# Attention placed ahead of block 3, and Strassen's scheme in the second product of blocks 3 to 5

## The chip, the core and the metric

The kernel runs on one core of one Trainium2 chip. The time is the device time of one execution, in microseconds (us): 510.04 us is the median of three runs of the kernel before (508.49 to 510.45). One further execution was profiled. Its page names the engines so: PE is the matrix engine's multiplications and PEld its weight loads, DVE the vector engine, ACT the scalar engine, POOL the general engine, SP the engine that issues most DMAs. One matrix instruction of this kernel covers 512 or 256 columns of one PSUM bank. PSUM has eight banks of 128 x 512 floats here.

## The reference

A linear attention with a decaying state gives one row per token; the rows of all heads are joined and go through a two-layer product with a gate between:

```
for t in range(S):                              # batch 4, heads 8, S = 768, D = 48
    cur = einsum('bhd,bhe->bhde', u * k_t, v_t)
    y[:, :, t] = einsum('bhd,bhde->bhe', r_t, state + cur)
    state = w_t * state + einsum('bhd,bhe->bhde', k_t, v_t)
x = y.transpose(0, 2, 1, 3).reshape(3072, 384)
h = x @ w_in                                    # 384 -> 2048
g = where(h >= 1, h, where(h <= -1, 0, (h + 1) ** 2 / 4))
out = g @ w_out                                 # 2048 -> 384
```

## The kernel before

**Tiling.** The 3072 tokens are twelve units of 256 (64 time steps of four batches). Attention is computed unit by unit (`attention`, line 498), since unit u needs the state after unit u-1. Two units make a block of 512 tokens, `x_[b % 2]`, and there are six blocks, 0 to 5. A block goes through 16 steps, one for each 128 of the 2048 hidden rows. In block 0 five of them and in block 1 fourteen are done as two halves of 256 columns (`HALVES`), so that the first unit of the block can be used alone.

**A step.** Every float is kept as a rounded high part and a low part, and a product of two floats is three products of parts. The first product of a step (`product_in`, line 1294; its matmul is line 1299) is 9 instructions of 512 columns into a bank `h`. The gate is two ACT operations and one DVE operation (lines 1111 to 1113), and ACT and DVE then make the two parts `gh` and `gl` (1115, 1116). The second product (`product_out`, matmul in line 1319) is again 9 instructions of 512 columns; they add into three banks `acc`, one for each 128 output rows, over all 16 steps. After the last step of a block the three banks are copied out (line 1136) and stored.

**Strassen's scheme.** Blocks in `FAST` take another path, `fast` (line 952); before, that is block 5 alone. It treats two steps as one 2 x 2 problem: the hidden rows of the two steps, the two halves of the 512 tokens, and the first two of the three output thirds (the last third is done plainly). Sums and differences of the gate's results (`t`, lines 989 to 997) and of the weights (`sums_of`, line 925, written once into buffers that attention no longer needs, `HOMES`) go in; seven products and four plain ones come out, `M1` to `M7`, `P`, `Q`, `R` in line 914. Every product is three instructions of 256 columns (line 1011). Of the eight pairs of a block, seven are done so with 33 instructions; the last pair is done plainly into the same places with 36. The results lie in five banks (3, 4, 5, 1, 2), and `finish` (line 1052) puts the outputs together with one ACT copy and six DVE additions, and stores six pieces of 128 KB.

**Attention of a unit.** SP loads w, r and k (as `wq`, `rk`), a token-major copy `nk` and v. DVE runs two scans for each of two slots (lines 543, 538), multiplies (564, 614), sums (604, 607), masks (590) and updates the state (671, 674); POOL multiplies (602, 610); PE does small products of 64 x 64 (584, 653, 696) and transposes (623). The result is evacuated as high part by ACT (768) and low part by DVE (766) into `x_`, a fourth slice into `last`, which six DMAs spread over the rest of `x_` (line 811). Each unit uses banks 0, 1 and 2 in turn (`take`) and one of the two `h` banks.

**What sets the order.** Nothing is scheduled on the chip. At build a planner (`Plan`, line 54) takes every operation with its engine, a cost, what it reads and writes, and a due time, simulates all engines, and writes down the order of each engine. Due times of steps come from `STEP`, those of a unit's attention from the block that reads it (`step_of`, line 1143). Where the planner sees PE idle it adds multiplications by zero (`kept_warm`, line 184). Each engine then runs its list in order and waits on semaphores. `guard` (line 829) reads each unit's w again, two ACT operations each, for a check of the inputs; its verdict decides at the end whether another path (`general`) is run.

Of the kernel before, what the change touches and what calls it, by code (L numbers as in the profile page):

```python
# [10 lines left out]
F32 = mybir.dt.float32  # L11
# [5 lines left out]
ALU = mybir.AluOpType  # L17
# [26 lines left out]
FAST = {NB - 1}  # L44
# [3 lines left out]
SCRATCH = 8192  # L48
# [300 lines left out]
STEP, FIRST, PACED = 4.9, 24.0, 4.6  # L349
ROUNDS = 1  # L350


def attention_moe(tc, a):
# [32 lines left out]
    vn = tiles(2, [128, 2, VW], F32, "vn")  # L386
# [12 lines left out]
    fl = tiles(FULL, [128, 768], F32, "fl")  # L399
# [98 lines left out]
    def attention(u, when):  # L498
# [255 lines left out]

        def yevac(g, part, what):
            yv = bank[by[g]].rearrange("p (a c t) -> p a c t", a=4, t=C)
            if what:
                yv = yv[:, 3]
                to = [last[:, n, :].rearrange("p (c g t) -> p c g t", c=2, g=2)[:, :, g, :] for n in range(2)]
            else:  # L760
                yv = yv[:, 0:3]
                to = [x[:, n].rearrange("p a (c g t) -> p a c g t", c=2, g=2)[:, :, :, g, :] for n in range(2)]
            if part and u in INPLACE:
# [16 lines left out]
        def names(what, n, g):  # L780
            return ("last" if what else ("x", blk % 2, half), n, g)
# [15 lines left out]
        for what in (0,) if alone else (1, 0):  # L797
            for g in range(2):
                op("ACT", 0.27 if what else 0.48, due, [("b", by[g])], [names(what, 0, g)], lambda g=g, w=what: yevac(g, 0, w))
                if u not in INPLACE:  # L800
# [8 lines left out]

        def fill(e, h, j):  # L810
            e.dma_start(
                out=x[64 * h + 48 : 64 * h + 64, :, j, :].bitcast(F32),
                in_=last[64 * h + 16 * j : 64 * h + 16 * j + 16].bitcast(F32),
            )

        xs = [(("x", blk % 2, half), n, g) for n in range(2) for g in range(2)]
        for j in range(0 if alone else 3):
            for h in range(2):
                e, how = (nc.scalar, "ACT") if h and u < APART else (nc.sync, "SP")
                op(how, 0.8 if how == "ACT" else 0.63, due, [("last", n, g) for n in range(2) for g in range(2)] + xs, [("x", blk % 2, half, j, h)],  # L820
                   lambda e=e, h=h, j=j: fill(e, h, j), size=32768)
        plan.group(first, when, LEADS.get(u, LEAD))
# [70 lines left out]
    for i in range(3):  # L893
        mem(("h", i, 0), None, ("gh", i))
        mem(("l", i, 0), None, ("gl", i))
    mem(("h", 0, 1), None, *xk)
    his = [gh, [xf[:, 512 * i : 512 * i + 512] for i in range(3)]]
    los = [gl, [xf[:, 1536 + 512 * i : 2048 + 512 * i] for i in range(3)]]
    HOMES = [("nk0", 1536, 0), ("nk0", 1536, 512), ("nk0", 1536, 1024), ("vn0", 800, 0), ("vn1", 800, 0), ("r0", 512, 0), ("r1", 512, 0),
             ("wq0", 521, 0), ("wq1", 521, 0), ("wq2", 521, 0), ("y0", 520, 0), ("seeds0", 520, 0), ("fl0", 768, 0), ("fl1", 768, 0),  # L900
             ("fl2", 768, 0), ("fl2", 768, 256)]
    olds = [ku_keys, (), (), (("v", 0), ("vpad", 0)), (("v", 1), ("vpad", 1)), (("R", 0),), (("R", 1),), (("w", 0),), (("w", 1),), (("w", 2),),
            ("y",), ("seeds",), (("fl", 0),), (("fl", 1),), (("fl", 2),), ()]
# [3 lines left out]
    def sums(i, n):  # L907
# [7 lines left out]
             "M5": (1, 0), "R": (1, 1), "M3": (2, 0), "M4": (2, 1)}  # L915
# [36 lines left out]
    def fast(n, after=()):  # L952
# [9 lines left out]
        for half in range(2):  # L962
            xs += [(("x", b % 2, half), i, g) for i in range(2) for g in range(2)]
            xs += [("x", b % 2, half, j, h) for j in range(3) for h in range(2)]
# [10 lines left out]
        def split(i, x, key):  # L975

            hi, lo = his[k][i], los[k][i]
            op("ACT", 0.6, due, [key], fresh_in(("h", i, k)), lambda: A.copy(hi, x))
            op("DVE", 0.67, due, [key, ("h", i, k)], fresh_in(("l", i, k)), lambda: V.tensor_tensor(
                out=lo, in0=x, in1=hi.bitcast(F32), op=ALU.subtract), port=True)  # L980
# [408 lines left out]
```

## Time and profile before

| what | value |
|---|---|
| median of three runs | 510.04 us |
| the profiled execution | 508.99 us, of which 507.3 us from its first to its last instruction (the span) |
| granted clock of the matrix engine, mean | 0.993 |
| DVE, ACT, POOL busy | 368.3, 299.9, 100.4 us |
| matmuls of the first product, 512 columns | 693; of 256 columns, 342 |
| matmuls of the plain second product, 512 columns | 549; of 256 columns, 342 |
| matmuls of Strassen's scheme, 256 columns | 267 |
| HBM read and written | 47.09 and 4.72 MB |

Matmul rows give how long each is under way, and they overlap: one of 512 columns is listed with about 0.4 us, while the next one starts after about 0.23 us. What an instruction costs the matrix engine is therefore read from the distance of starts in a row of them. DVE and ACT rows overlap by some hundredths of a microsecond in the same way, and the busy times count no moment twice. In the windows view, each row is a stretch of the span with the busy time of each engine in it and, in brackets, the number of instructions.

### The profile page before, as it was taken

The numbers are of one execution on the slowest core, as the hardware profiler recorded it, in microseconds if no ns is written. First come the engines' busy times: TensorE is split into PE (matmuls) and PEld (weight loads), VectorE is DVE, ScalarE is ACT, GpSimd is POOL, SyncE is SP. The second block draws the span as 40 slices with busy tenths as digits, with TensorE's granted clock in tenths as the row PEclk, the third lists the DMA queues.
The fourth block names the chain that finished last, engine by engine and source line by source line (L and its number), as shares of the span: only waits on it lengthen the run. The fifth ranks groups of instructions, "written<-read, shape, count | busy, mean of one in ns | idle before, by whom it ended". The sixth has DMA issues, their size and how long they took to land. (4 is left out here: it accounts for less than half of the span.)

```text
span 507.3 us, 13117 instructions
## 1 busy us (share of the span) xinstructions
PE 492.1 (97%) x5525; PEld 417.2 (82%) x5525; DVE 368.3 (73%) x631; ACT 299.9 (59%) x628; POOL 100.4 (20%) x80
## 2 busy tenths in 40 slices
PE   6989999999999999999999999999999999999995
PEld 4679988888999998888888888888788877889894
DVE  6999989988888797835888435987333486697753
ACT  4769798978754566634555543556444454665651
POOL 1745516411121103101110101110000034402000
PEclk9989999999999999999999999999999999999998
DMA  8984916156342352501442201430100020100002
GB/s 295 378 317 154 364 79 232 57 172 216 105 153 92 127 165 71 167 1 67 151 152 59 109 0 59 157 121 12 63 0 1 1 58 13 68 1 2 1 1 68
DMA packets 22051, 54.70 MB, mean 108 GB/s; under 512 B 3040, under 2 KB 9184, under 8 KB 21984
## 3 DMA queue, kind: packets, MB, share of 16 engines
q1 hardware_dynamic: 21840, 53.65, 30.7%
q8 instruction: 45, 0.74, 0.6%
q14 instruction: 22, 0.18, 0.1%
q10 hardware_dynamic: 144, 0.13, 0.1%
HBM read 47.09 MB, written 4.72 MB: 102 GB/s over the span
## 5 line engine op out<-in xcount | busy, mean ns | idle before, releaser
L1299 PE MATMUL h<-x,wt 128*128 128x512 f32 (+1 forms) x1035 | 219.6, 360 | 1.5 <-DVE g L1113 0.8
L1299 PEld LDWEIGHTS h<-x,wt 128*128 128x128 f32 x1035 | 169.9, 188 | 32.6 <-DVE g L1113 1.8
L1319 PE MATMUL acc<-gh,wt 128*128 128x512 f32 (+1 forms) x594 | 130.3, 354 | 0.0
L1319 PEld LDWEIGHTS acc<-gh,wt 128*128 128x128 f32 x594 | 97.2, 188 | 16.8
L1111 ACT ACTIVATE g<-h 128x512 f32<-128x512 f32 (+1 forms) x99 | 51.0, 515 | 96.1 <-PE h L1299 86.6
L1113 DVE SCALAR_TENSOR_TENSOR g<-g,h 128x512 f32<-128x512 f32 (+1 forms) x99 | 57.1, 579 | 65.3 <-ACT g L1112 57.5
L1116 DVE TENSOR_TENSOR gl<-g,gh 128x512 fp32r<-128x512 f32 (+1 forms) x99 | 62.2, 634 | 22.9 <-ACT gh L1115 20.4
L1319 PE MATMUL acc<-gl,wt 128*128 128x512 f32 (+1 forms) x297 | 72.1, 351 | 0.0
L1115 ACT CAST gh<-g 128x512 fp32r<-128x512 f32 (+1 forms) x99 | 52.7, 536 | 26.7 <-DVE g L1113 23.0
L610 POOL TENSOR_TENSOR r<-cst,d 128x512 f32<-128x512 f32 x18 | 19.2, 1089 | 194.2 <-PE bank L696 158.0
L1319 PEld LDWEIGHTS acc<-gl,wt 128*128 128x128 f32 x297 | 50.3, 188 | 8.4
L1112 ACT ACTIVATE g<-g 128x512 f32<-128x512 f32 (+1 forms) x99 | 54.3, 550 | 1.8
L478 POOL TENSOR_SCALAR wraw<-fl 128x768 uint16<-128x768 f32 x13 | 43.3, 3354 | 50.1 <-ACT wraw L476 38.7
L602 POOL TENSOR_TENSOR nk<-nk 128x768 f32<-128x768 f32 x9 | 17.6, 1961 | 83.3 <-DMA nk<-in_nk 83.3
L543 DVE TENSOR_TENSOR_SCAN p<-wq,seeds 128x520 f32<-128x520 f32 x24 | 30.1, 1254 | 3.0 <-DMA wq<-in_w 2.1
L538 DVE TENSOR_TENSOR_SCAN y<-wq,seeds 128x520 f32<-128x520 f32 x24 | 30.0, 1250 | 0.8
L972 DVE SCALAR_TENSOR_TENSOR rk<-rk,h 128x512 f32<-128x512 f32 x16 | 11.0, 685 | 14.5 <-ACT rk L971 14.4
L590 DVE COPY_PREDICATED r<-below,bank 128x512 f32<-128x512 int32 x23 | 16.0, 730 | 4.6 <-PE bank L584 4.5
L564 DVE TENSOR_TENSOR rk<-rk,y 128x512 f32<-128x512 f32 x24 | 18.0, 750 | 0.9 <-ACT nk L554 0.7
L768 ACT CAST x<-bank 128x384 fp32r<-128x384 f32 x24 | 11.1, 485 | 12.0 <-PE bank L696 11.8
L969 ACT ACTIVATE rk<-h 128x512 f32<-128x512 f32 x16 | 9.6, 598 | 13.9 <-PE h L1299 13.9
L696 PEld LDWEIGHTS bank<-rk,st 64*64 64x64 f32 (+1 forms) x704 | 12.2, 133 | 6.7 <-issue 5.0
(198 smaller groups left out, 619.9 us busy)
## 6 DMA issues: line engine op xcount, KB each, us to landing
rk<-in_rk SPq DMA_DIRECT2D x24, 512.0 KB, 4.9
wraw<-in_wbits SPq DMA_DIRECT2D x16, 768.0 KB, 7.6
nk<-in_nk SPq DMA_DIRECT2D x9, 768.0 KB, 4.5
wq<-in_w SPq DMA_DIRECT2D x24, 260.5 KB, 2.8
vn<-in_v SPq DMA_DIRECT2D x12, 384.0 KB, 6.7
fl<-in_w SPq DMA_DIRECT2D x12, 260.0 KB, 2.9
out_y<-g SPq DMA_DIRECT2D x10, 256.0 KB, 3.1
x<-last SPq DMA_DIRECT2D x60, 32.0 KB, 3.1
```

Of the source, the lines that this page charges most:

```text
L478: op(on, 0.62 if f in SIGNS else 3.2, due, [("fl", k)], [("raw", f)], lambda: e.tensor_scalar(out=half(1), in0=s, scalar1=0.0, scalar2=327 ...
L538: V.tensor_tensor_scan(out=y_[:, ::-1], data0=w[:, SEG:0:-1], data1=sv[:, ::-1], initial=0.0, op0=ALU.mult, op1=ALU.add)
L543: V.tensor_tensor_scan(out=pv[:, q].rearrange("p n c -> p (n c)"), data0=w[:, 0:SEG], data1=sv, initial=0.0, op0=ALU.mult, op1=ALU.add,)
L564: op("DVE", 0.69, due, ["y"], [("k", s)], lambda q=q: V.tensor_tensor(out=parts(q, 1), in0=parts(q, 1), in1=y_.rearrange("p (n c) -> p n c ...
L610: op("POOL", 1.1, due, ["d", "cst"], [("R", h)], lambda h=h: G.tensor_tensor(out=r_[h], in0=twice.unsqueeze(1).unsqueeze(1).broadcast_to([ ...
L1111: op("ACT", c, due, [("h", n)], [("g", gk)], lambda: nc.scalar.activation(gs, hs(), AF.Relu, scale=0.5, bias=0.5), uses=[hk])
L1112: op("ACT", c, due, (), [("g", gk)], lambda: nc.scalar.activation(gs, gs, AF.Square))
L1113: op("DVE", 0.13 + 0.53 * k, due, [("h", n)], [("g", gk)], lambda: nc.vector.scalar_tensor_tensor(out=gs, in0=gs, scalar=1.0, in1=hs(), op ...
L1115: op("ACT", c, due, [("g", gk)], [("gh", gk)], lambda: nc.scalar.copy(ghs, gs))
L1116: op("DVE", 0.17 + 0.54 * k, due, [("g", gk), ("gh", gk)], [("gl", gk)], lambda: nc.vector.tensor_tensor(out=gls, in0=gs, in1=ghs.bitcast( ...
L1299: nc.tensor.matmul(hp, lhsT=wx[f][:, cs], rhs=xt[:, j, :], start=n == 0, stop=n == 8)
L1319: nc.tensor.matmul(o[j], lhsT=wx[f][:, cs], rhs=gt, start=first and i == 0, stop=stop and i == 2, skip_group_check=True)
```

## The change

Five things change. Their names: `xf` are two new f32 tiles for the x of blocks 4 and 5; `FLAT` holds those blocks; `ADDED` says at which block's first step each unit's attention is given to the planner, and `PULLED` gives units 4 to 11 due times 16 us apart, the last at the start of block 3.

```
-FAST = {NB - 1}
+FAST = set(range(NB - 3, NB))
+FLAT = {NB - 2, NB - 1}
...
-SCRATCH = 8192
+SCRATCH = 2048
...
+PITCH = 16.0
+SLOW, QUICK = 5.75, 4.05
+ADDED = {0: (2, 3), 1: (4, 5), 2: tuple(range(6, NU))}
...
+    xf = tiles(len(FLAT), [128, 3, WIDE], F32, "xf")
...
             if flat_x:
+                A.copy(to[0].bitcast(F32), yv)
...
-        t += STEP if cs is whole else STEP / 2 if n >= HALVES[0] else PACED
+        pace = QUICK if b in FAST else SLOW
+        t += pace if cs is whole else pace / 2 if n >= HALVES[0] else PACED
...
+    PULLED = {u: (before_fast((NU - 1 - u) * PITCH), 4.0) for u in range(4, NU)}
...
-             "M5": (1, 0), "R": (1, 1), "M3": (2, 0), "M4": (2, 1)}
+             "M5": (1, 0), "R": (1, 1), "M3": (2, 0), "M4": (0, 0)}
...
+        xs += [("hu", u) for u in range(1, NU - 1)]
...
-            multiply(1.2, one_, [("M3", S3, g1), ("M4", lambda: weights(f0, A2), g0)])
-            multiply(1.3, two_, [("M2", lambda: weights(f1, A1), g2), ("Q", lambda: weights(f1, A3), g2)])
-            multiply(1.3, two_, [("M5", lambda: weights(f1, A2), g3), ("R", lambda: weights(f1, A3), g3)])
-            multiply(1.3, two_, [("M3", S5, g3), ("M4", lambda: weights(f1, A2), g2)])
+            multiply(1.2, one_, [("M3", S3, g1)])
+            multiply(1.2, one_, [("M4", lambda: weights(f0, A2), g0)])
+            turn = ["turn"] if b == NB - 1 else []
+            multiply(1.3, two_, [("M5", lambda: weights(f1, A2), g3), ("R", lambda: weights(f1, A3), g3)], False, *turn)
+            multiply(1.3, two_, [("M2", lambda: weights(f1, A1), g2), ("Q", lambda: weights(f1, A3), g2)], False, *turn)
+            multiply(1.3, two_, [("M3", S5, g3)], False, *turn)
+            multiply(1.3, two_, [("M4", lambda: weights(f1, A2), g2)], False, *turn)
...
-        sum2(e3, 2, eq[:, 0:3:2], both, ["x", "u3"], [("g", 2)], 0.69)
+        sum2(e3[:, 0], 2, eq[:, 0], 0, (), ["ea"], 0.42)
+        sum2(e3[:, 1], 0, eq[:, 2], 0, (), ["u3"], 0.42)
...
+    def divided(b):
+        for half in range(2):
+            src, x = xf[b % 2][:, :, halves[half]], x_[b % 2][:, :, :, halves[half]]
...
+            op("ACT", 0.82, due, srcs, [(("x", b % 2, half), 0, g) for g in range(2)], lambda src=src, x=x: A.copy(x[:, 0], src))
+            op("DVE", 0.94, due, [*srcs, *((("x", b % 2, half), 0, g) for g in range(2))], [(("x", b % 2, half), 1, g) for g in range(2)],
+               lambda src=src, x=x: V.tensor_tensor(out=x[:, 1], in0=src, in1=x[:, 0].bitcast(F32), op=ALU.subtract), port=True)
...
-            for u in (2 * b + 2, 2 * b + 3):
-                attention(u, step_of(u))
-            if b + 1 in FAST:
+            for u in ADDED.get(b, ()):
+                attention(u, *PULLED.get(u, (step_of(u), None)))
+            if b == min(FAST):
...
+                    load(due, w.rearrange("p (n c) -> p n c", c=C), a["w"][u, q][:, 0:SEG].rearrange("p (n c) -> p n c", c=C + 1)[:, :, 1:],
+                         ["guard", *fresh_in("guard")])
+                    guard(w, "guard", i, due)
+            if b + 1 in FLAT:
+                divided(b + 1)
```

Blocks 3, 4 and 5 all go through `fast`. All of attention is ordered ahead of block 3's Strassen products, which now also name every unit's state product (`hu`) as something they come after. The x of units 8 to 11 is evacuated once, as f32, into `xf`, and is divided into high and low part shortly ahead of its block (`divided`: two ACT and two DVE operations for a block). `M4` moves to bank 0, so that six banks are in use, and the last pair's products are ordered bank by bank. The scheme's scratch lies in buffers that attention and the plain blocks leave (`nk`, `g`, `vn`, `st`, `fl`); the buffers `fl` and `vn` become one tile each. The extra loads of w for the check go into `last` in runs of 64 floats, in block 3 and 4, where they went into the three `fl` buffers.

On the matrix engine, here is the order behind the last unit's products (the rows with 64x64; `acc` are banks 3 to 5, `gh` and `gl` the parts of the gate's result, `wt` the weights, `kt_again` the parts of a pair's first quarter). Before, unit 11 ends in block 4, between plain second products:

```order
L1319 MATMUL acc1_112<-gh2_103,wt12_1244 128x512
L1319 MATMUL acc2_113<-gh2_103,wt12_1244 128x512
L1319 MATMUL acc0_111<-gl2_106,wt12_1244 128x512
L1319 MATMUL acc1_112<-gl2_106,wt12_1244 128x512
L1319 MATMUL acc2_113<-gl2_106,wt12_1244 128x512
L1299 MATMUL h1_115<-x0_95,wt15_1367 128x512 x9
```

Of the change, where unit 11 ends when three first products of block 3 (hidden rows 0 to 2) have been issued:

```order
L703 MATMUL bank2_117<-r1_90,vn0_85 64x64
L1348 MATMUL h0_113<-x1_95,wt3_587 128x512 x9
L1042 MATMUL acc0_110<-kt0_again_4108,wt0_356 128x256 x6
L1042 MATMUL acc1_111<-gh0_100,wt1_365 128x256 x2
L1042 MATMUL acc1_111<-gl0_103,wt1_365 128x256
```

The second products of blocks 3 and 4, in rows of 512 columns before, are rows of 256 columns now, and no attention stands between them.

On DVE, at the end of block 3 (L1136 is the copy of one output bank, L1116 a low part). Before, with unit 11's masks (L590) behind it:

```order
L1113 SCALAR_TENSOR_TENSOR g1_99<-g1_99,h0_114 128x512
L1116 TENSOR_TENSOR gl1_105<-g1_99,gh1_102 128x512
L1113 SCALAR_TENSOR_TENSOR g0_98<-g0_98,h0_114 128x512
L1136 COPY ob0_107<-acc0_111 128x512
L590 COPY_PREDICATED r0_90<-below0_71,bank1_117 128x512
L590 COPY_PREDICATED r1_91<-below0_71,bank2_118 128x512
```

Of the change (L1097 are the additions of `finish`, L1131 is `divided`, L1004 the gate, L1010 and L1020 low parts):

```order
L1097 TENSOR_TENSOR p0_86<-acc2_112,p0_86 128x256
L1010 TENSOR_TENSOR g1_again_4286<-rk1_82,nk0_again_4252 128x512
L1004 SCALAR_TENSOR_TENSOR rk0_81<-rk0_81,h1_114 128x512
L1097 TENSOR_TENSOR xf0_108<-acc2_112,p0_86 128x256
L1131 TENSOR_TENSOR x1_95<-xf1_109,x1_95 128x3x256
L1020 TENSOR_TENSOR kt0_again_4108<-rk0_81,kt0_again_4108 128x256
L1097 TENSOR_TENSOR xf0_108<-bank1_116,p0_86 128x512
L1097 TENSOR_TENSOR xf0_108<-bank1_116,xf0_108 128x256
L1097 TENSOR_TENSOR xf0_108<-acc1_111,p0_86 128x512
L1097 TENSOR_TENSOR xf0_108<-bank2_117,xf0_108 128x256
L1097 TENSOR_TENSOR xf0_108<-bank0_115,xf0_108 128x256
```

One copy has become seven additions, with the division of block 5's x among them.

On the matrix engine, at the very end of the program. Before, banks 4, 2 and 1 take the products of hidden rows 14, then the same banks those of 15:

```order
L1011 MATMUL acc1_112<-x0_95,wt14_1344 128x256 x6
L1011 MATMUL bank2_118<-x0_95,fl2_again_5241 128x256 x3
L1011 MATMUL bank2_118<-x0_95,wt14_1344 128x256 x3
L1011 MATMUL bank1_117<-x0_95,wt14_1344 128x256 x6
L1011 MATMUL acc1_112<-x0_95,wt15_1367 128x256 x6
L1011 MATMUL bank1_117<-x0_95,wt15_1367 128x256 x6
L1011 MATMUL bank2_118<-x0_95,fl2_again_5241 128x256 x3
L1011 MATMUL bank2_118<-x0_95,wt15_1367 128x256 x3
```

Of the change, the last seven rows, all of hidden rows 15:

```order
L1042 MATMUL acc1_111<-nk0_again_4252,wt15_1330 128x256 x2
L1042 MATMUL acc1_111<-g1_again_4286,wt15_1330 128x256
L1042 MATMUL bank2_117<-nk0_again_4252,st0_again_4671 128x256
L1042 MATMUL bank2_117<-nk0_again_4252,st1_again_4683 128x256
L1042 MATMUL bank2_117<-g1_again_4286,st0_again_4671 128x256
L1042 MATMUL bank0_115<-nk0_again_4252,wt15_1330 128x256 x2
L1042 MATMUL bank0_115<-g1_again_4286,wt15_1330 128x256
```

Bank 1 is complete first, then 4, 2 and 0; the last two banks hold a half each.

More of the change, by code (lines that the diff above doesn't have):

```diff
@@ L385, in attention_moe @@
     nk = one([128, 2, 2, DM], F32, "nk")
-    vn = tiles(2, [128, 2, VW], F32, "vn")
+    v2 = one([128, 2, 2, VW], F32, "vn")
+    vn = [v2[:, i] for i in range(2)]
     p_ = one([128, 4 * NC, C + 1], F32, "p")
@@ L398, in attention_moe @@
     ob = one([128, WIDE], F32, "ob")
-    fl = tiles(FULL, [128, 768], F32, "fl")
+    f3 = one([128, FULL, 768], F32, "fl")
+    fl = [f3[:, i] for i in range(FULL)]
+    xf = tiles(len(FLAT), [128, 3, WIDE], F32, "xf")
     acc = tiles(3, [128, WIDE], F32, "acc", psum)
@@ L496, in take, with attention @@
         return state["bank"]
-    def attention(u, when):
+    def attention(u, when, lead=None):
         if u == EARLY:
@@ L780, in names @@
         def names(what, n, g):
-            return ("last" if what else ("x", blk % 2, half), n, g)
+            return ("last" if what else ("xf" if flat_x else "x", blk % 2, half), n, g)
         def spread(g):
@@ L812, in fill @@
                 out=x[64 * h + 48 : 64 * h + 64, :, j, :].bitcast(F32),
-                in_=last[64 * h + 16 * j : 64 * h + 16 * j + 16].bitcast(F32),
+                in_=last[64 * h + 16 * j : 64 * h + 16 * j + 16, 0:parts_x].bitcast(F32),
             )
-        xs = [(("x", blk % 2, half), n, g) for n in range(2) for g in range(2)]
+        xs = [(xk, n, g) for n in range(parts_x) for g in range(2)]
         for j in range(0 if alone else 3):
@@ L819, in attention @@
                 e, how = (nc.scalar, "ACT") if h and u < APART else (nc.sync, "SP")
-                op(how, 0.8 if how == "ACT" else 0.63, due, [("last", n, g) for n in range(2) for g in range(2)] + xs, [("x", blk % 2, half, j, h)],
-                   lambda e=e, h=h, j=j: fill(e, h, j), size=32768)
-        plan.group(first, when, LEADS.get(u, LEAD))
+                op(how, 0.8 if how == "ACT" else 0.63, due, [("last", n, g) for n in range(parts_x) for g in range(2)] + xs, [(*xk, j, h)],
+                   lambda e=e, h=h, j=j: fill(e, h, j), size=16384 * parts_x)
+        plan.group(first, when, LEADS.get(u, LEAD) if lead is None else lead)
         for q in range(2):
@@ L887, in attention_moe @@
     ku_keys = "nk", ("ku", 0), ("ku", 1)
+    mem("guard", None, *(("last", n, g) for n in range(2) for g in range(2)))
     mem("hq", None, ("kt", 0), ("kt", 1))
+    mem("e1", None, *((("xf", 0, half), 0, g) for half in range(2) for g in range(2)), *(("xf", 0, half, j, h) for half in range(2) for j in range(3) for h in range(2)))
     def first_hl(k):
@@ L963, in fast @@
             xs += [(("x", b % 2, half), i, g) for i in range(2) for g in range(2)]
-            xs += [("x", b % 2, half, j, h) for j in range(3) for h in range(2)]
+            xs += [("x", b % 2, half, j, h) for j in range(3) for h in range(2) if b not in FLAT]
+        xs += [("hu", u) for u in range(1, NU - 1)]
         step_ops.append(len(plan.ops))
@@ L1010, in accumulate, with multiply @@
                 for wi, gi in ((0, 0), (1, 0), (0, 1)):
-                    PE.matmul(bank[i][:, half * UT : half * UT + UT], lhsT=w[wi], rhs=g[gi], start=i not in opened, stop=True,
+                    PE.matmul(bank[i][:, half * UT : half * UT + UT], lhsT=w[wi], rhs=g[gi], start=(b, i) not in opened, stop=True,
                               skip_group_check=True)
-                    opened.add(i)
-        def multiply(late, reads, todo, fresh=False):
-            banks = {("b", PLACE[to][0]): 0 for to, _, _ in todo}
+                    opened.add((b, i))
+        def multiply(late, reads, todo, fresh=False, *turn):
+            banks = {("b", PLACE[to][0]): 0 for to, _, _ in todo} | {key: 0 for key in turn}
             op("PE", 0.351 * len(todo), (n, -late * STEP - 0.1), reads, list(banks), lambda: accumulate(todo), fresh=fresh, code=6 * len(todo))
```

100 lines of the change are left out of this document (57 added, 43 removed).

## The prediction

> **What bounds the kernel now.** I read the page first, for the shares and the slices.
>
> ```profile
> span 507.3 us, 13117 instructions
> PE 492.1 (97%) x5525; PEld 417.2 (82%) x5525; DVE 368.3 (73%) x631; ACT 299.9 (59%) x628; POOL 100.4 (20%) x80
> PE   6989999999999999999999999999999999999995
> DVE  6999989988888797835888435987333486697753
> PEclk9989999999999999999999999999999999999998
> ```
>
> PE is full in nearly every slice and its clock is granted. A pipelined PE shows as full even where it starts less than it could, so I asked for the groups of instructions by form and for who waited for whom.
>
> ```profile
> L1299 PE MATMUL h<-x,wt 128*128 128x512 f32 x693 | 173.2, 397 | 0.5 <-DVE g L1113 0.5
> ACT g L1111 <- PE h L1299: 86.6, 65, 4.3
> DVE g L1113 <- ACT g L1112: 57.5, 45, 4.7
> ```
>
> PE stood idle for 0.5 us ahead of 693 instructions, while ACT waited 86.6 us for PE. So PE sets the time, and a change is worth the matrix work it takes away, as long as the other engines still feed PE. For the work I need the distance of starts, from the timeline of block 5 (the only block with Strassen's scheme now): two first products, then 33 half-width products, then the next first product.
>
> ```profile
> 446.17 4.36 PE L1299 MATMUL h<-x,wt 128*128 128x512 f32 x18
> 450.37 0.39 PE L1011 MATMUL bank<-gh,wt 128*128 128x256 f32 x2
> ...
> 453.89 0.52 PE L1011 MATMUL bank<-x,wt 128*128 128x256 f32 x3
> 454.24 1.09 PE L1299 MATMUL h<-x,wt 128*128 128x512 f32 x4
> ```
>
> 18 full-width products take 450.37 - 446.17 = 4.20 us, 0.2333 each. The 33 half-width ones take 454.24 - 450.37 = 3.87 us, 0.1173 each.
>
> **The gain.** A pair of steps costs 18 x 0.2333 = 4.20 us in the plain second product and 3.87 in the scheme: 0.33 less. The last pair of a block has 36 half-width products, 4.22, so 0.02 more. Blocks 3 and 4 change over: 14 pairs x 0.33 less 2 x 0.02 is 4.6 us. If half a width costs exactly half, three products of 0.1167 go in each of 14 pairs, and it is 4.9. I take **4.7**. First products, attention's products and the weight splits on PE are the same in number; two rows of filling by zeros fewer in the start are worth nothing that I can see.
>
> **Does DVE keep up while attention is drawn together?** This is the step on which all hangs. Attention's DVE work of units 6 to 11 now has to be done in blocks 1 and 2. I compare when PE wants unit 11 with when DVE can have done it. Before, PE came to its last part (the products with r) here:
>
> ```profile
> 423.51 0.69 PE L696 MATMUL bank<-rk,st 64*64 64x64 f32 x32
> ```
>
> By the order of the engine, 98 first and 95 second products stood ahead of this before, 70 and 67 now. 56 x 9 products x 0.2333 = 117.6 us have moved behind it, so PE would come to it at 423.5 - 117.6 = **305.9 us** if nothing held it up. DVE's work up to unit 11's last mask, from the windows:
>
> ```profile
> 0.00:420.00 420.00, 411.11 (x4928) 346.55 (x4929) 311.99 (x527) 254.70 (x544) 85.55 (x59) 1.00 0.37 126
> 0.00:100.00 100.00, 92.52 (x1339) 77.83 (x1340) 91.52 (x140) 78.82 (x150) 47.42 (x28) 0.98 0.64 237
> 100.00:200.00 100.00, 99.11 (x1394) 92.35 (x1393) 82.43 (x158) 65.38 (x174) 16.57 (x12) 1.00 0.44 141
> 380.00:400.00 20.00, 20.00 (x87) 16.06 (x86) 6.50 (x10) 9.26 (x15) 0.00 (x0) 1.00 0.00 1
> 0.00:420.00 420.00, 2.41 (x7) 3.20 (x5) 1.00 0.37 126
> L766 DVE TENSOR_TENSOR x<-bank,x 128x384 fp32r<-128x384 f32 x22 | 11.9, 551 | 7.4 <-ACT last L768 4.8 <-ACT x L768 2.5
> L766 DVE TENSOR_TENSOR last<-bank,last 128x128 fp32r<-128x128 f32 x20 | 5.4, 281 | 1.2 <-ACT last L768 0.8 <-PE acc L1319 0.3
> ```
>
> Up to 420 us DVE (third pair of a row) was busy 311.99 us. From it go the weight sums already begun (2.41, the fifth row, of line 933 alone); 29 steps that now come later (96 low parts ahead of the last mask before, 67 now), at 6.50 us in 20 quiet us, so 1.37 for a step of 4.20: 39.6; and the low-part evacuations of units 8 to 11, 8 x 0.551 + 8 x 0.281 = 6.7. That leaves 263.3 us of DVE work by 305.9 us. The first 100 us are about as before (91.52 done), so 171.8 us of work stand in 205.9 us: **DVE must hold 83.4%**. It held 91.5% in the first 100 us and 82.4% in the second, with PE at 99.1 there. In that second stretch PE was full all the same, so DVE was not asked for more. So 83.4% is near what the trace shows, with little to spare. Nothing below zero comes of it, since PE can't be freed further; at 91.5% DVE is 18 us early, at 82.4% it is 171.8 / 0.824 - 205.9 = 2.6 us late. I take 0, since the nearest row of a crowded stretch, 91.5%, lies above, and keep both ends.
>
> POOL shares these stretches with DVE.
>
> ```profile
> L602 POOL TENSOR_TENSOR nk<-nk 128x768 f32<-128x768 f32 x9 | 17.6, 1961 | 83.3 <-DMA nk<-in_nk 83.3
> L610 POOL TENSOR_TENSOR r<-cst,d 128x512 f32<-128x512 f32 x18 | 19.2, 1089 | 194.2 <-PE bank L696 158.0 <-DVE d L607 36.2
> L1116 DVE TENSOR_TENSOR gl<-g,gh 128x512 fp32r<-128x512 f32 x61 | 45.2, 744 | 20.6 <-ACT gh L1115 18.1 <-PE acc L1319 2.4
> L979 DVE TENSOR_TENSOR gl<-rk,gh 128x512 fp32r<-128x512 f32 x12 | 8.1, 684 | 0.3 <-ACT gh L978 0.3
> ```
>
> The same subtraction takes 744 ns among attention and 684 in block 5: 0.06 x 61 = 3.7 us of DVE time in all, and it is in the sums above. [...]
>
> **The other edits.** The division of x, two ACT and two DVE operations for each of two blocks, has its nearest rows in the weights' split:
>
> ```profile
> L470 ACT CAST wt<-fl 128x768 fp32r<-128x768 f32 x14 | 11.4, 829 | 2.7 <-DVE fl L480 2.6
> L483 DVE TENSOR_TENSOR wt<-fl,wt 128x768 fp32r<-128x768 f32 x16 | 15.0, 942 | 0.0
> ```
>
> That is 3.3 us of ACT and 3.8 of DVE, in blocks 3 and 4. What hides it: the stage windows of block 5 as it is.
>
> ```profile
> 440.00:460.00 20.00, 20.00 (x121) 17.58 (x120) 17.41 (x36) 13.88 (x26) 2.93 (x5) 1.00 0.11 41
> 480.00:500.00 20.00, 20.00 (x137) 18.38 (x136) 11.18 (x21) 9.70 (x17) 0.00 (x0) 1.00 0.01 2
> ```
>
> With weight sums among its work DVE is at 87% and PE full; without them at 56%. Block 3 takes over those sums, blocks 4 and 5 don't have them. I take 0, and 2 us for the uncovered case. At the ends of blocks 3 and 4 `finish` holds banks that the next block wants, for about seven DVE additions (0.42 to 0.69 us by the rows below, 3.5 us). Between the last product of the old block and the first into the first contested bank stand two first products and six half-width ones at least: 2 x 2.10 + 0.70 = 4.9 us. I take 0; uncovered, about 3 us for each end, 6. The twelve loads for the check go as runs of 256 bytes; behind each wait two ACT operations, and behind these ACT's gates. The rows:
>
> ```profile
> fl<-in_w SPq DMA_DIRECT2D x12, 260.0 KB, 2.9
> vn<-in_v SPq DMA_DIRECT2D x12, 384.0 KB, 6.7
> ```
>
> The load as it was takes 2.9 us, the one with the shorter runs 6.7. ACT is busy 46 to 49% in the quiet windows, so I take 0. At 6.7 each could stop ACT for 3.8 us, of which one first product covers 2.1: 12 x 1.7 = 20 us at worst.
>
> **The end.**
>
> ```profile
> 500.36 0.42 DVE L1063 TENSOR_TENSOR ob<-bank,rk 128x256 f32<-128x256 f32 x1
> 500.52 0.51 PE L1011 MATMUL bank<-x,wt 128*128 128x256 f32 x3
> 500.70 0.68 DVE L1063 TENSOR_TENSOR rk<-bank,p 128x512 f32<-128x512 f32 x1
> 501.47 0.69 DVE L1063 TENSOR_TENSOR g<-bank,rk 128x512 f32<-128x512 f32 x1
> 502.19 0.42 ACTq L1078 DMA_DIRECT2D out_y<-g  x1
> 502.34 0.41 SPq L1078 DMA_DIRECT2D out_y<-g  x1
> ```
>
> Behind the last product, at 501.03, DVE needs until 502.16, and two stores go out together. Now the last addition is two of 0.42 and the stores alternate between two queues. DVE's chain is as long (0.42 + 0.42 for 0.69), the first of the last stores is 0.4 us earlier: I take 0.1 off, between 0.4 more and 0.4 less.
>
> **Sum.** 508.99 (the profiled execution, 1.7 us more than its span) - 4.7 - 0.1 = 504.2. It lay 1.05 us below the median of the runs, 510.04; on that scale it is **505.2 us**, and with the bounds of gain, end and the runs' own spread 503 to 507.3.
>
> **Rivals.**
>
> *DVE a little late ahead of block 3*: it holds 80.5 to 83.4%, so that 0 to 7.4 us come back. At the 82.4% of the second hundred, 505.2 + 2.6 = 507.8; range 507 to 512.6. For it: the need lies just above that row, and DVE's list is in order, so that one late load or product holds up all behind it. Against: DVE was idle there while PE set the pace.
>
> *DVE becomes the bound*, in the same place: masks, scans and state updates of six units run back to back with the steps, each waiting for PE's small products and for loads into buffers just left. Below 80.5% the change is slower than before by over 0.5%; at 78%, 171.8 / 0.78 - 205.9 = 14.4 us, **519.6**. For it: the rows of 200 us and later never show DVE above what PE asks. Against: 91.5% in the first hundred, with the weights' decoding besides.
>
> *Waits at block ends or behind the check's loads*, up to 6 and 20 us: 508 to 525. Against: ACT at half its time.
>
> *Weight loads decide.* Each half-width product has a load of its own, so a pair has 51 loads for 36. By the windows above, loads are 18.38 of 20 us busy in block 5, against 16.06 in the quiet plain one. If the 2 x (7 x 15 + 18) = 246 more were laid bare at the group's 188 ns,
>
> ```profile
> L1011 PEld LDWEIGHTS bank<-x,wt 128*128 128x128 f32 x45 | 6.3, 188 | 0.3
> ```
>
> it is 46 us more, 551. But the distance of 0.1173 us contains them. [...]
>
> **Chances.** Forecast 0.64; DVE a little late 0.20, of which 0.04 still end faster; DVE the bound 0.10; block ends or loads 0.05, of which 0.03 slower; weight loads 0.01. Faster by over 0.5% (2.6 us, about what a measurement of this kernel can tell from no change): 0.64 + 0.04 = 0.68. Within: 0.16 + 0.02 = 0.18. Slower: 0.10 + 0.03 + 0.01 = 0.14. A range from 503 to 511.5 leaves out about 0.2: all that is slower, and a little at each side.
>
> **What would show it.** Right: 33 half-width products between first products in blocks 3 and 4 in 3.87 us; unit 11's last products at about 306 us; the last product of all at about 496. The DVE share from 100 to 306 us at 83 to 84%, PE's windows full. Wrong: PE waiting for masks (line 590 before) or for r ahead of 306 us; gaps of PE at two block ends; ACT idle behind the loads into `last`.

## The result, and the profile after

| kernel | median | profiled execution | span | matmuls of Strassen's scheme |
|---|---|---|---|---|
| before | 509.26 us (4 runs, 507.0 to 510.45) | 508.99 us | 507.3 us | 267 |
| after | 502.68 us (4 runs, 502.04 to 504.18) | 502.04 us | 500.5 us | 801 |

The ratio is 0.988, with a 95% interval of 0.9836 to 0.9925: 6.6 us less, where 4.8 were forecast. The direction came as predicted; the time lies 0.3 us below the low end of the range. Of the 2.5 us between the forecast 505.2 and the measured time, 0.8 is the scale: with a fourth run the median of the kernel before is 509.26 where the forecast had 510.04. The other 1.8 us are the question, and whether DVE had the reserve that the forecast gave it.

The page of the kernel after: its span, the busy times, two rows of the 40 slices, and the group of the first product.

```profile
span 500.5 us, 13728 instructions
PE 486.8 (97%) x5767; PEld 426.3 (85%) x5767; DVE 402.8 (80%) x702; ACT 314.3 (63%) x658; POOL 102.5 (20%) x80
PE   6989999999999999999999999999999999999994
DVE  6999999997787898898979988787877575675563
L1348 PE MATMUL h<-x,wt 128*128 128x512 f32 (+1 forms) x1035 | 221.4, 362 | 2.2 <-DVE x L779 1.4
```

PE is full as before; DVE rose from 73% to 80% of the span, most of it in the middle (178.37 us from 100 to 304 us, where it had 150.86). What PE waited for after the start, from 30 us on (releaser, us in total, times, longest), first before, then after:

```profile
PE bank L584 <- DVE rk L614: 1.8, 1, 1.8
PE h L1299 <- DVE g L1113: 0.8, 2, 0.5
PE h L1299 <- DVE r L590: 0.4, 1, 0.4
```

```profile
PE h L1348 <- DVE st L678: 0.4, 1, 0.4
PE h L1348 <- DVE g L1159: 0.3, 1, 0.3
```

In the kernel after 0.7 us are left in 470 us, none of them at a block's end, behind a load for the check or behind the division of x. For those three terms, each taken as 0, the view shows no wait. The timeline of PE at the passage into block 3 (start, length, engine, line, operation) shows two things at once:

```profile
303.47 1.11 PE L703 MATMUL bank<-r,vn 64*64 64x64 f32 x64
304.52 2.35 PE L1348 MATMUL h<-x,wt 128*128 128x512 f32 x9
306.71 0.86 PE L1042 MATMUL acc<-kt_again,wt 128*128 128x256 f32 x6
...
308.82 2.26 PE L1348 MATMUL h<-x,wt 128*128 128x512 f32 x9
310.92 0.40 PE L1042 MATMUL bank<-gh,wt 128*128 128x256 f32 x2
...
313.40 2.26 PE L1348 MATMUL h<-x,wt 128*128 128x512 f32 x9
315.50 0.40 PE L1042 MATMUL acc<-nk_again,wt 128*128 128x256 f32 x2
...
318.69 4.36 PE L1348 MATMUL h<-x,wt 128*128 128x512 f32 x18
```

The last row of unit 11's products (`r,vn`) starts at 303.47 us and the next first product at 304.52. The row that the forecast put at 305.9 us, `rk,st` just ahead of it, starts at 302.96, 2.9 us earlier. And 18, 21 and 27 half-width products take 308.82 - 306.71, 313.40 - 310.92 and 318.69 - 315.50: together 66 in 7.78 us, 3.89 for 33, forecast 3.87. The windows of the crowded stretch (PE, PEld, DVE, ACT, POOL busy, clock, DMA share, GB/s):

```profile
100.00:304.00 204.00, 203.72 (x3194) 176.89 (x3195) 178.37 (x316) 113.81 (x280) 41.14 (x33) 1.00 0.37 122
180.00:320.00 140.00, 139.97 (x2217) 116.03 (x2216) 124.91 (x209) 82.83 (x190) 32.19 (x30) 1.00 0.35 116
```

DVE held 178.37 / 204 = 87.4% with PE full, where the forecast asked for 83.4%; in the second stretch, which the experiments come back to, it was busy 124.91 of 140 us. The end, from the timeline: DVE's last two additions, behind the last product at 494.19.

```profile
493.74 0.68 DVE L1097 TENSOR_TENSOR xf<-acc,p 128x512 f32<-128x512 f32 x1
493.91 0.28 PE L1042 MATMUL bank<-g_again,wt 128*128 128x256 f32 x1
494.34 0.75 DVE L1097 TENSOR_TENSOR xf<-bank,xf 128x256 f32<-128x256 f32 x2
```

From the last product to the end of the span are 6.29 us; before they were 6.31. So all 6.8 us of the shorter span lie ahead of the last product.

**A ledger for PE.** To see where, I split the moment of the last product in two: the products at a fixed distance (0.2333 us for 512 columns, as block 5 showed before; for 256 half of that, 0.1167, where block 3 shows 0.118; attention's small ones by their own distance), and PE's time beyond its products. The products come to 465.2 us before and 460.3 after: 4.9 less. The time beyond them went from 35.6 to 33.6 us. That second part, 2 us, is what the experiments had to explain. The table at the end of the next section gives it, in three stretches, for the kernels that differ by the scheme or the draw.

### The profile page after: what moved, and what is told of

It reads as the page before. It is cut to its first block, busy times and chain, and to the rows that moved or that the text cites. A ratio compares the mean times of both kernels' runs of the same rounds, so it can differ in the third digit from the quotient of the medians.

```text
span 500.5 us, 13728 instructions
## 1 busy us (share of the span) xinstructions
PE 486.8 (97%) x5767; PEld 426.3 (85%) x5767; DVE 402.8 (80%) x702; ACT 314.3 (63%) x658; POOL 102.5 (20%) x80
## 4 chain that ended last, share of the span: by engine, by line
PE 92%; DVE 4%; issue 2%; DMA 1%; ACT 1%; SPq 0%; DVEq 0%; ACTq 0%
PE h L1348 41%; PE acc L1368 21%; PE acc L1042 10%; PE bank L1042 9%; PE bank L703 4%; PE bank L591 3%; PE bank L630 2%; PE bank L660 1%; DVE fl L487 1%; DMA cst<-in_consts 1%; DVE y L545 1%; DVE r L597 0%; DVE rk L571 0%; PE h L660 0%; DVE wt L490 0%
## 5 line engine op out<-in xcount | busy, mean ns | idle before, releaser
L1368 PE MATMUL acc<-gh,wt 128*128 128x256 f32 (+1 forms) x402 | 80.0, 334 | 0.0
L1368 PEld LDWEIGHTS acc<-gh,wt 128*128 128x128 f32 x402 | 61.3, 188 | 7.8
L1004 DVE SCALAR_TENSOR_TENSOR rk<-rk,h 128x512 f32<-128x512 f32 x48 | 32.8, 684 | 36.3 <-ACT rk L1003 36.0
L1157 ACT ACTIVATE g<-h 128x256 f32<-128x256 f32 (+1 forms) x67 | 31.8, 475 | 46.5 <-PE h L1348 41.4
L1159 DVE SCALAR_TENSOR_TENSOR g<-g,h 128x256 f32<-128x256 f32 (+1 forms) x67 | 35.2, 528 | 12.6 <-ACT g L1158 11.2
L1368 PE MATMUL acc<-gl,wt 128*128 128x256 f32 (+1 forms) x201 | 44.5, 329 | 0.0
L1161 ACT CAST gh<-g 128x256 fp32r<-128x256 f32 (+1 forms) x67 | 32.9, 498 | 13.4 <-DVE g L1159 7.9
L617 POOL TENSOR_TENSOR r<-cst,d 128x512 f32<-128x512 f32 x18 | 21.6, 1222 | 90.2 <-PE bank L703 46.8
L1162 DVE TENSOR_TENSOR gl<-g,gh 128x256 fp32r<-128x256 f32 (+1 forms) x67 | 39.0, 591 | 1.0 <-ACT gh L1161 0.6
L1158 ACT ACTIVATE g<-g 128x256 f32<-128x256 f32 (+1 forms) x67 | 33.9, 511 | 1.0
L550 DVE TENSOR_TENSOR_SCAN p<-wq,seeds 128x520 f32<-128x520 f32 x24 | 30.8, 1284 | 3.1 <-DMA wq<-in_w 2.2
L1003 ACT ACTIVATE rk<-rk 128x512 f32<-128x512 f32 x48 | 30.4, 633 | 0.9
L1010 DVE TENSOR_TENSOR gl<-rk,gh 128x512 fp32r<-128x512 f32 x36 | 25.8, 720 | 4.1 <-ACT gh L1009 3.9
L1010 DVE TENSOR_TENSOR g_again<-rk,nk_again 128x512 fp32r<-128x512 f32 x33 | 23.3, 710 | 6.8 <-ACT nk_again L1009 6.5
```

Of the source, the lines that this page charges most:

```text
L1004: op("DVE", 0.66, due, [("h", n)], [qk], lambda: V.scalar_tensor_tensor(out=gf, in0=gf, scalar=1.0, in1=bank[plan.given[hk]], op0=ALU.min, ...
L1157: op("ACT", c, due, [("h", n)], [("g", gk)], lambda: nc.scalar.activation(gs, hs(), AF.Relu, scale=0.5, bias=0.5), uses=[hk])
L1158: op("ACT", c, due, (), [("g", gk)], lambda: nc.scalar.activation(gs, gs, AF.Square))
L1159: op("DVE", 0.13 + 0.53 * k, due, [("h", n)], [("g", gk)], lambda: nc.vector.scalar_tensor_tensor(out=gs, in0=gs, scalar=1.0, in1=hs(), op ...
L1161: op("ACT", c, due, [("g", gk)], [("gh", gk)], lambda: nc.scalar.copy(ghs, gs))
L1162: op("DVE", 0.17 + 0.54 * k, due, [("g", gk), ("gh", gk)], [("gl", gk)], lambda: nc.vector.tensor_tensor(out=gls, in0=gs, in1=ghs.bitcast( ...
```

## The experiments

A kernel with more than one run comes with its ratio to the kernel before as that ran beside it. The medians come from several chips, and that kernel's median went from 508.75 to 510.3 us among them, so between two medians of different groups of runs about 1 us is unsure.

**One part alone: the earlier attention, and block 4.** In `e1_early_only` everything of the change stays but the scheme is left to block 5; in `e2_early_fast45` it is left to blocks 4 and 5. So "the earlier attention" here stands for all that is not the scheme: the f32 x with its division and the new end are in it too.

```
-FAST = set(range(NB - 3, NB))
+FAST = {NB - 1}                 # e2: {NB - 2, NB - 1}
-        t = dues[start_of[min(FAST)]] - us
+        t = dues[start_of[NB - 3]] - us
```

> Of the change, only block 5 keeps Strassen's scheme; attention still ends ahead of block 3 and x of blocks 4 and 5 still waits as f32. Theory A (of the 6.6 us gained, 4.6 to 4.9 are fewer products in blocks 3 and 4, and 2.0 are waits of the matrix engine around attention that the earlier order takes away): about 2 us below before, near 507.3 us, span near 505.3; the matrix engine's time above its products as in the change, 33.6 us. Theory B (the products give all of it, 3.3 us for each block, and the order gives nothing): 509.3 us, span 507.3. Theory C (crowding attention costs time, which the products hide): over 510 us.

> Of the change, block 3 goes back to plain second products; blocks 4 and 5 use Strassen's scheme. Theory A: one block's share back, 2.3 to 2.5 us over the change, near 505.0 us, span near 502.9. Theory B: 3.3 us over the change, near 506.0.

Measured: 507.93 us (12 runs; ratio 0.9968, 0.9948 to 0.9988) and 504.7 us (ratio 0.9915, 0.9887 to 0.9943). From no early block to two, the median falls by 3.2 and 2.0 us and the products' sum in the ledger by 2.5 and 2.4. Both blocks together give 507.93 - 502.68 = 5.25 us by the medians and 4.5 by the ratios (0.9968 and 0.988), so the two changed blocks don't seem to carry all of the 6.6. The earlier attention by itself seemed to give 1.3. Of the theories, A came nearest in both runs, and B, all by the products, fails in both.

**Another order for the same work.** The planner shakes its keys by random numbers and keeps its best order. Begun from another number (`SEED`), it writes another order for the same instructions. If times hang on that, the 1.3 us may be nothing but the order that was drawn.

```
-BACK, SHAKES, SHAKE, SEED = 4, 40, 0.7, 1
+BACK, SHAKES, SHAKE, SEED = 4, 40, 0.7, 2
```

> The kernel before, with another seed for the planner's 40 shaken orders; the work is the same. If the 2 us beyond the products were the luck of one search (theory D), this run moves by about 2 us from 509.3 either way. Theory A: within 1 us of 509.3, since attention still stands where its block's due time puts it.

> The change, with another seed for the planner's shaken orders; the work is the same. Theory A: within 1 us of 502.7. Theory D (luck of the search): near 504.7.

Measured: the kernel before 509.6 us (ratio 1.0016, 0.9997 to 1.0035), the kernel after 504.41 us (0.9916, 0.9883 to 0.9948). By the medians the same work in another order cost the kernel after 1.7 us more, near theory D, but the intervals of the two ratios (0.9836 to 0.9925 with draw 1) overlap. The kernel before shows no difference that can be told, as theory A expected. Two draws say little about a scatter, so a third followed, and a second one of the earlier attention alone.

> The changed kernel with the planner's draw begun from 3 in place of 1: the same work, another order. Theory P: the products give 4.7 to 5.2 us and the earlier attention some 1.3 more whatever the plan, so the run lies 6 us or more below the kernel before with the same draw (next run): 502 to 503.7. Theory L: the order itself gives nothing, and what goes beyond the products is the scatter of plans (with draw 2 the kernel after took 504.4): anything from 502 to 506.

> The kernel before with the planner's draw begun from 3. It gave 509.2 with draw 1 and 509.6 with draw 2. Theory P: 509 to 510, with PE's starts falling behind by 2 us or more around attention after 100 us, and 6 us or more above the kernel after with this draw. Theory L: 508 to 511, and the distance to the kernel after with this draw 3 to 6 us, so that the mean distance of three draws (6.6 and 5.2 for the first two) comes to about 5.

> The changed kernel with the scheme in block 5 alone and the earlier attention kept, with the planner's draw begun from 2. With draw 1 it took 507.9. It does the work of the kernel before; with draw 2 that one took 509.6 and the kernel after 504.4. Theory P: 508 to 508.5, again 1.3 below the kernel before with its own draw. Theory L: 509.1 to 509.6 or more, no better than the kernel before. The products of blocks 3 and 4 are this run less the kernel after with draw 2: both theories 4.6 to 5.2, so a distance outside 3.5 to 6 shows how far the scatter of plans hides them.

Measured: after 504.64 us (0.9895, 0.9863 to 0.9927), before 505.89 us (0.9928, 0.9896 to 0.996), the earlier attention alone with draw 2 508.67 us (0.9987, 0.9961 to 1.0013). The middle one decides: **the kernel before, with nothing changed but the order drawn, is 3.4 us faster** than the 509.26 of above, and 3.95 us faster than draw 1 as it ran beside it (median 509.84), with an interval that lies clear of no change. No theory had that. Theory P falls: with draw 3 the change is worth 505.89 - 504.64 = 1.25 us, not 6. Theory L had the kind right and the size too small. The earlier attention with draw 2 lies between what the two expected. Between kernels with the same number of the draw, the scheme in blocks 3 and 4 gives 508.67 - 504.41 = 4.26 us with draw 2 and 5.25 with draw 1; by the ratios, 3.6 and 4.5. The same number isn't the same order, though: with other work the planner writes another one, so these differences hold the scatter of orders too.

One more draw was picked by the planner's own reckoning, to see whether that tells good orders from bad ones, and as a possible better version.

> The changed kernel with the planner's draw begun from 11, whose plan ends earliest in the planner's own reckoning of the draws looked at. That reckoning gives 496.2 for it; 496.7, 499.3 and 500.1 for the kernel after with draws 1, 2, 3 (spans 500.5, 502.6, 503.9); 502.6, 502.6 and 501.8 for the kernel before with them (spans 507.3, 507.1, 504.0). Theory R: the planner's reckoning tells plans of one kernel apart, so this one comes out at the changed kernel or a little below, 501.5 to 503, PE's time beyond its products 33 to 34 us. Theory S: the scatter is in what the planner doesn't know, so this one lies like any other draw around the mean of three, 504, from 502 to 506, as likely above the kernel after with draw 2 as below.

Measured: 502.62 us (ratio 0.9868, 0.9836 to 0.9899), span 500.4. That is as theory R says, though theory S allowed 502 to 506 and isn't ruled out by one draw; and it is no better than the kernel after: nothing tried beats that one by more than a measurement tells. In the numbers of that expectation, the reckoning puts the four orders of the kernel after as the chip does. Of the kernel before it names the best one too, but puts it 0.8 us ahead where the spans are 3.1 and 3.3 apart.

**How much reserve has DVE?** The scan of line 545 is run again in units 6 to 11, with the order of all engines left as it is: for one of a unit's two slots (six scans, about 7.3 us of DVE), for both (twelve, 14.6), and twice more for both (24, 29.3). The repeated scan writes the same values.

```
+                for _ in range(2 if u > 5 and q else 1):   # e6: 2 if u > 5; e7: 3 if u > 5
-                V.tensor_tensor_scan(
+                  V.tensor_tensor_scan(
```

> The change in its own order on every engine; in units 6 to 11 one of the two backward scans is done twice on DVE (same result, unknown to the planner): 6 x 1.22 = 7.3 us more DVE work between about 180 and 300 us, where DVE is now idle 11.6 us of 120. Theory A (DVE was idle there because the matrix engine set the pace, so its lists stand ahead of need): 0 to 1 us more than the change, 502.7 to 503.7. Theory E (DVE is the bound there and its idle time is made of waits that can't be used): 7.3 us more, 510.

> As the run before, with both backward scans of units 6 to 11 done twice: 14.6 us more DVE work. DVE has 11.6 us of idle time in 180 to 300 us. Theory A: 3 to 5 us more than the change, 506 to 508, since 3 us don't fit. Theory E: 14.6 us more, 517.

> As before, with both backward scans of units 6 to 11 done three times: 29.3 us more DVE work. Theory A: at least 29.3 - 11.6 = 17.7 us more than the change, 520 to 523, with DVE at 97% or more in 180 to 320 us. Theory E: 29.3 us more, 532.

Measured: 505.98 us (ratio 0.9952, 0.9926 to 0.9978), 511.11 us (1.0034, 1.0 to 1.0068) and, in a single run, 526.71 us; against the kernel after 3.3, 8.4 and 24.0 us more. Each lies between what theories A and E expected, so neither has it right. The stretch from 180 to 320 us, in the columns as above, of the three:

```profile
180.00:320.00 140.00, 137.67 (x2198) 113.10 (x2197) 131.26 (x213) 81.31 (x189) 30.62 (x25) 1.00 0.37 117
```

```profile
180.00:320.00 140.00, 132.96 (x2154) 107.67 (x2153) 131.61 (x204) 76.35 (x180) 29.10 (x24) 0.99 0.35 114
```

```profile
180.00:320.00 140.00, 123.85 (x1925) 99.50 (x1925) 134.46 (x197) 68.80 (x165) 24.71 (x17) 0.98 0.33 108
```

DVE goes from 124.91 us in the kernel after to 131.26, 131.61 and 134.46 of 140: with this order it got no higher than 94 to 96%. PE, full in the kernel after, falls to 137.67, 132.96 and 123.85. Its waits in the last of the three, for the same stretch, name the place:

```profile
PE h L1349 <- DVE st L679: 7.0, 3, 4.2
PE h L1349 <- DVE g L1160: 6.1, 4, 3.7
PE h L1349 <- DVE seeds L550: 2.0, 1, 2.0
```

First products wait for the update of the state (`st`) and for a gate (`g`) queued behind attention's work on DVE: ahead of the gate of the longest such wait, 3.7 us, stand three runs of one scan, 3.79 us. So the reserve is about 4 us (7.3 put in, 3.3 came out) to 6 us (14.6 and 8.4; 29.3 and 24.0): neither none nor enough to swallow a dozen scans. The long waits also come with a lower clock here. In the kernel after and in the first of the three, whose longest wait for `st` or `g` is 1.1 us, the granted clock of the stretch is 1.00; in the second, with a wait of 2.8 us, it is 0.99, and in the third, with 3.7 and 4.2 us, 0.98 (0.99 and 0.97 from 180 to 300 us). Within the rounding of these figures that is 0.7 to 2.1 and 3.0 to 3.5 us of PE, of the 8.4 and 24.0. The rival of DVE as the bound was real, a few microseconds away.

**The end alone.** `e8_tail_old` puts `M4` back into its old bank and the last addition into one piece; the order bank by bank and the stores on two queues stay as in the change.

```
-             "M5": (1, 0), "R": (1, 1), "M3": (2, 0), "M4": (0, 0)}
+             "M5": (1, 0), "R": (1, 1), "M3": (2, 0), "M4": (2, 1)}
...
-        sum2(e3[:, 0], 2, eq[:, 0], 0, (), ["ea"], 0.42)
-        sum2(e3[:, 1], 0, eq[:, 2], 0, (), ["u3"], 0.42)
+        sum2(e3, 2, eq[:, 0:3:2], both, (), ["ea", "u3"], 0.69)
```

> Of the change, M4 goes back to bank 2 and the last addition of a block is one of two halves again. The part that is asked for is the stretch from the end of the last product to the end of the span: 6.3 us in the kernel before and in the change. If the order by banks is worth the 0.1 us of the prediction: 6.4 us. If it is worth 0.5 us and other things ate it: 6.8 us. The total may move by 2 us either way, since the planner makes another order.

Measured, in a single run: 507.67 us, span 506.1. From the last product to the end of the span it is 6.33 us against 6.29. The kernel after and the three runs with repeated scans have the same order there and took 6.29, 5.76, 6.33 and 6.11 us, so 0.04 us can't be told from nothing. The 5.6 us by which the span is longer lie elsewhere. The edit gave the planner another problem and so another order: at 100 us of this kernel its first products already stand some 4 us behind those of the kernel after. Its windows in the start (the third number from the end is the granted clock) tell most of that:

```profile
10.00:15.00 5.00, 5.00 (x80) 3.95 (x78) 4.18 (x6) 3.27 (x6) 0.00 (x0) 0.66 1.05 417
30.00:35.00 5.00, 3.03 (x14) 3.03 (x15) 4.76 (x8) 0.91 (x2) 3.29 (x1) 0.62 0.77 281
35.00:40.00 5.00, 5.00 (x84) 4.47 (x84) 3.35 (x5) 3.57 (x8) 2.56 (x1) 0.69 0.27 108
```

The clock lost 5 x (0.34 + 0.38 + 0.31) = 5.15 us there, against 1.75 in the kernel after (last section): 3.4 us of the 5.6. A small edit in a planned kernel moves everything else too, and what it is worth itself is read at its place, not from the total.

**The ledger of all.** Times in us; "beyond" is PE's time beyond its products, from the profiled execution, up to 40 us, from there to 150, and from 150 to the last product. Each row is one execution, and what the clock loses in the start (last section) is in the column to 40 us.

| kernel, draw | median | span | products | beyond: to 40 | 40 to 150 | 150 on |
|---|---|---|---|---|---|---|
| before, 1 | 509.26 | 507.3 | 465.2 | 25.6 | 4.4 | 5.6 |
| before, 2 | 509.6 | 507.1 | 465.2 | 26.0 | 3.5 | 5.8 |
| before, 3 | 505.89 | 504.0 | 465.2 | 23.1 | 3.4 | 5.1 |
| attention early, 1 | 507.93 | 505.2 | 465.2 | 25.1 | 3.1 | 5.2 |
| attention early, 2 | 508.67 | 506.9 | 465.2 | 25.0 | 3.6 | 6.7 |
| and block 4, 1 | 504.7 | 503.6 | 462.7 | 27.3 | 1.8 | 5.7 |
| after, 1 | 502.68 | 500.5 | 460.3 | 24.8 | 2.5 | 6.3 |
| after, 2 | 504.41 | 502.6 | 460.3 | 26.1 | 3.3 | 6.4 |
| after, 3 | 504.64 | 503.9 | 460.3 | 25.6 | 3.6 | 7.9 |
| after, 11 | 502.62 | 500.4 | 460.3 | 24.4 | 3.4 | 5.7 |

Only the products' column follows the change, and it does so by its making: it is a count of instructions times a distance, and that the distance holds in block 3 is what the 3.89 us show. The start goes from 23.1 to 27.3 whatever the change, and from 150 us on no kernel with the attention early is better than the best of those before. The 2 us between the first row and "after, 1" are 0.8 gained in the start and 1.9 from 40 to 150 us, less 0.7 lost behind.

## Why the prediction was right, and where not

*PE sets the time.* Right. PE is full in the windows of the kernel after from 100 to 320 us, and from 30 us on no wait of PE is longer than 0.4 us.

*The products give 4.7 us (4.6 to 4.9).* Right. The instructions sum to 4.9 less, 33 half-width ones take 3.89 us, and the scheme put in alone gives 5.25 and 4.26 by the medians, 4.5 and 3.6 by the ratios. That the first two average 4.75 is luck in part, since the order scatters by more.

*DVE keeps up, at 83.4%, taken as 0.* Right in the sign and for the reason given, that 82.4% of the second hundred microseconds was what was asked and not what DVE can do. The need was put too low: by 304 us DVE had done 269.99 us of work, 87.4% from 100 us on, where 263.3 were put down. A part of that is a slip in the sum. It takes off 16 low-part evacuations, 6.7 us, from the work up to 420 us, but four of them came only behind 423 us, 1.7 us. Then 2.5 us of weight sums, taken off as later work, and 3.5 of block 3's own first DVE operations stand ahead of 304 us in the kernel after. And some operations took longer than before, one of the two scans and a step of the state's update among them (before, then after, with POOL's product with `r` behind them):

```profile
L543 DVE TENSOR_TENSOR_SCAN p<-wq,seeds 128x520 f32<-128x520 f32 x24 | 30.1, 1254 | 3.0 <-DMA wq<-in_w 2.1
L674 DVE TENSOR_TENSOR st<-st,ptot 128x384 f32<-128x384 f32 x20 | 11.6, 607 | 0.1
```

```profile
L550 DVE TENSOR_TENSOR_SCAN p<-wq,seeds 128x520 f32<-128x520 f32 x24 | 30.8, 1284 | 3.1 <-DMA wq<-in_w 2.2
L681 DVE TENSOR_TENSOR st<-st,ptot 128x384 f32<-128x384 f32 x20 | 14.2, 732 | 0.1
L617 POOL TENSOR_TENSOR r<-cst,d 128x512 f32<-128x512 f32 x18 | 21.6, 1222 | 90.2 <-PE bank L703 46.8
```

That step of the state's update takes 732 ns where it took 607, a scan 1284 where it took 1254, and POOL's product 1222 where it took 1089. Why they took longer, no run here takes apart. POOL was busy for 41.14 us of the stretch from 100 to 304 us, where it had 26.27, and PE was full all the same (203.72 of 204). The forecast's "18 us early" at 91.5% was too kind. The scans put the reserve at 4 to 6 us.

*Division of x, block ends, loads for the check: 0 each.* Right, by the waits above. The worst case of the loads rested on the shorter runs costing 6.7 us each; the row of the kernel after is

```profile
last<-in_w SPq DMA_DIRECT2D x12, 256.0 KB, 2.9
```

the same 2.9 us as the old load of 260.0 KB. *The end: 0.1.* It is 0.02 between the two kernels and 0.04 by the edit alone, within the bounds given; but executions with one order of the end differ by 0.6 us, so the runs can't show a term of 0.1.

*The step that failed* is the sentence that nothing below zero comes of drawing attention together, "since PE can't be freed further", and with it the range, whose low end counted only the bounds of the products, the end and the spread of runs. PE had 35.6 us beyond its products, 10 of them after 40 us, and a new order moves these. How much without any change in the work, the draws show: the three orders of the kernel before give 509.26, 509.6 and 505.89 us, mean 508.25; those of the kernel after 502.68, 504.41 and 504.64, mean 503.91. The means are 4.3 us apart, near the products' share; with three draws a side, 2.1 and 1.1 us of scatter leave that uncertain by about 1.3. Draw 1, the one that both kernels happen to have, is 1.0 us above the mean for the one and 1.2 below it for the other, and 4.3 + 1.0 + 1.2 are the 6.6 us, but for rounding. That is arithmetic and not a cause: what is shown is that the order alone moves a kernel by as much as the 2 us beyond the forecast, so that these are most likely the order that was drawn. A range for this kernel needed some 2 us more at both ends.

*What stays open:* whether the earlier attention is worth something of its own. With draws 1 and 2 it took 1.3 and 0.9 us off the kernel before; with draw 3 the whole change was worth less than the products alone. Three draws, 2 to 4 us apart, can't settle 1 us. Open too is what in an order costs or saves the time outside the start.

## What to carry to other kernels

Where a planner or a search writes the order, any edit draws a new order of everything; so time two or three draws of both kernels before a difference of half a per cent is put down to the edit (here the order alone moved one by 3.4 us of 509.26), and read the edit's own worth at its place in the trace. An engine's share in a stretch where another sets the pace is what was asked of it, and says nothing about its reserve (from 100 to 304 us DVE had 74.0% before and 87.4% after, PE over 99% both times): repeat one of its instructions until the other engine begins to wait, and the reserve is known in microseconds (here 4 to 6). A change that removes work from the engine that sets the time gives about that work's distance of starts, here 4.9 us in the sum and 3.6 to 5.3 in the runs, as long as the waits view stays nearly empty.

## What the hardware showed beside

**A fall of the clock in the start.** PE sits idle at about 28 us, for x of the first unit (1.44 us in the kernel after, 0.95 in the kernel before with draw 3), or, in the kernel before with draw 1, for 1.84 us ahead of 31.76, for `rk` (the row of 1.8 us of its waits above). In 11 of the 14 profiled executions the windows of 5 us between 25 and 40 us have a granted clock below 1.00, down to 0.50. PE's timeline and the windows (the clock again third from the end), first after, then the kernel before with draw 3:

```profile
28.53 3.80 PE L1348 MATMUL h<-x,wt 128*128 128x256 f32 x17 [1.44 <-DVE x L779]
```

```profile
28.28 2.25 PE L1299 MATMUL h<-x,wt 128*128 128x256 f32 x17 [0.95 <-DVE x L766]
```

```profile
25.00:30.00 5.00, 3.17 (x72) 2.77 (x73) 4.97 (x10) 2.23 (x3) 0.88 (x1) 0.85 1.03 413
30.00:35.00 5.00, 4.92 (x88) 4.48 (x87) 4.11 (x8) 3.64 (x8) 3.35 (x2) 0.80 0.98 367
```

```profile
25.00:30.00 5.00, 3.36 (x79) 3.02 (x80) 4.88 (x9) 3.44 (x7) 2.22 (x2) 1.00 1.02 401
30.00:35.00 5.00, 4.75 (x125) 3.31 (x127) 4.88 (x8) 4.16 (x8) 5.00 (x2) 1.00 1.02 420
```

The same 17 products take 3.80 us in the one and 2.25 in the other. The clock lost is 5 x (0.15 + 0.20) = 1.75 us of PE, that is 3.5 us at half speed: in windows of 1 us from 28 us on the clock is 0.77, 0.50, 0.50 and 0.52, then 1.00 again (the window from 30 to 35 us of `e4_after_seed2` has 0.50). In the same way the windows between 25 and 40 us give 1.75 and 1.70 us lost in the kernel before with draws 1 and 2, 3.45 with draw 2 of the kernel after, and none with draw 3 of either. `e2_early_fast45`, which had idled for 2.2 us just there, has 1.00 there too, but 0.66 at 10 to 15 us, behind an idle time of 2.1 us. `e5_scan_half`, whose order is that of the kernel after up to unit 6, lost about twice as much as that one:

```profile
25.00:30.00 5.00, 3.17 (x71) 2.77 (x72) 4.97 (x10) 2.26 (x3) 0.95 (x1) 0.79 1.02 408
30.00:35.00 5.00, 5.00 (x80) 4.66 (x80) 2.99 (x5) 3.11 (x6) 3.05 (x2) 0.53 1.00 339
```

5 x (0.21 + 0.47) = 3.4 us. So executions of one order differ here by 1.7 us, about as much as the runs of one kernel do (502.04 to 504.18 us for the kernel after). What sets the moment and the length of a fall, no run here shows. That the fall takes 1.75 us out of the start of the kernel before and none with draw 3 is read from the clock, and the wait of 1.84 us ahead of it isn't there with draw 3 either; that this explains the whole of that kernel's 3.4 us is not, since 40 to 150 us are better there too, by 1.0 us. Nor does the clock sort the draws: the six runs of the kernel after with draw 3 have mean clocks of 0.997 to 0.999, where the four with draw 1 have 0.991 to 0.995, and they are slower.

**Half-width products** with a weight load each kept to 0.118 us (66 in 7.78 us, in block 3).
